# Transposes of half-width column blocks, and their first visit moved ahead of the head sums

## The chip, the cores and the metric

The kernel runs on one core of a Trainium2 chip. The core has a matrix engine (TensorE, in the profile PE, with its weight loads as PEld), three engines for elementwise work (VectorE or DVE, ScalarE or ACT, GpSimd or POOL), a sync engine (SP) that issues DMAs here, and 16 DMA engines. The engines run their own instruction streams in order and wait for each other by semaphores. The metric is the time of one execution on the device in microseconds (us); lower is better. The kernel before takes 361.32 us, the median of three runs (360.48 to 361.93).

## The reference: sliding-window attention with a distance penalty, then a gated feed-forward block

The inputs are q, k and v of 8 batches, 8 heads, 576 tokens and 64 features per head, and three weight matrices. All are float32; the kernel computes in bf16 with float32 accumulation.

```python
scores = scale * np.matmul(q, k.transpose(0, 1, 3, 2))
rel = pos[:, None] - pos[None, :]
bias = slopes[:, None, None] * (-np.abs(rel))[None, :, :]
mask = (rel >= 0) & (rel < 128)
scores = np.where(mask, scores + bias[None], -1e9)
attn = softmax(scores)                      # over the keys
x = matmul(attn, v)                         # to 4608 tokens x 512 features
gelu(x @ w_gate) * (x @ w_val) @ w_out      # 512 -> 1536 -> 512
```

A token sees itself and the 127 tokens before it, so of the 576 x 576 scores only a band is computed.

## The kernel before

**Data and stages.** For each batch the kernel loads q, k and v with tokens on the partitions: `qs` and `ks` hold five blocks of token rows, four of 128 rows and a last one of 64, each 512 wide (8 heads of 64 features). Two buffers of each alternate by batch, `qs[b % 2]`. Scores need the features on the partitions, so TensorE transposes each block by a matmul with the identity: `qT` and `kT` hold, for each of four column groups c (128 columns, two heads), the 576 tokens along the free dimension. From there: score matmuls (`scores`, `scores2`, L209 and L291) into PSUM, exponentials by ACT (L222), multiplication with the precomputed penalty mask by DVE (L225), sums over the keys per head (`sums4`, L430, which reads `T`, a folded copy of the probabilities made by `add`), reciprocals by DVE (L435), and a way of these reciprocals through DRAM to all partitions (`gather` and `spread_dma`, two DMA issues each on ACT's queue, L443 and L449). The values (`values`, L494) are scaled on the way out of PSUM into `xT` (L558).

**The feed-forward part** runs over nine groups g of 512 tokens. For each group and each of twelve column blocks f, `gate_val(g, f)` issues eight matmuls of 512 columns into two PSUM banks (L625); ACT applies the gelu to one (L632) and DVE multiplies it with the other into `hid` (L633). The output matmuls (`out_part`, L662) follow.

**The order.** Everything is issued in the order in which the Python code runs; there is no planner behind it, and each engine keeps that order. The main loop interleaves attention of later batches with the feed-forward part of earlier tokens: in group g the loop over f issues `gate_val(g, f)` and, behind certain f, attention work of batches g + 1 and g + 2; behind the loop stand the steps of `steps(g)`, with the scores of batch g + 2 among the output matmuls. For groups 2 to 5 it goes so: behind f = 3 (4 in group 2) `sums4(g + 1)`, behind f = 5 (6) `gather(g + 1)`, behind f = 6 two transposes of batch g + 2, behind f = 7 (8) `spread_dma(g + 1)`, behind f = 8 the other two transposes, behind f = 9 the loads of q and k of batch g + 3 and of v of batch g + 2, issued by POOL. Batches 2 and 3 are transposed in group 1, behind f = 5, 7 and 11 and twice among the output steps, there directly ahead of score matmuls. Batch 1 has its own code (`transpose`, `transpose_runs`, L154); it transposes 64 columns at a time.

**PSUM banks.** There are eight; `bank()` hands them out in turn. `transposes(b, c)` takes one bank for q and one for k, writes five transposes into each and has the bank copied out by ACT (q) or DVE (k), 576 columns in one copy (L181). TensorE can write a bank again when the copy or the gelu and multiplication that read it are done.

**Forms.** The profile gives each matmul the part of the array that it uses, as rows*columns: 128*128 for the gate and output matmuls, 64*64 for scores and values, 128*32 for the head sums. The transposes of L178 have 128*128 for the blocks of 128 token rows and 64*128 for the last block.

Of the kernel before, what the change touches and what calls it, by code (L numbers as in the profile page):

```python
# [32 lines left out]
def kernel(  # L33
# [10 lines left out]
    nc = tc.nc  # L44
    B, H, S, D = q.shape
# [22 lines left out]
    def bank():  # L68
        return psum.tile([128, 512], FP32, name="ps")
# [11 lines left out]
    ident = consts.tile([128, 128], BF16, name="ident")  # L81
# [20 lines left out]
    def rows(j):  # L102
        return 64 if j == 4 else 128
# [12 lines left out]
    def load_qk(b):  # L116
        load(qs[b % 2], q, b)
        load(ks[b % 2], k, b)

    def load_v(b, js=range(5)):  # L120
        load(vb[b % 2], v, b, js, 64)
# [44 lines left out]
    def transpose(b, what, c, copy):  # L166
        ps = bank().bitcast(BF16)
        for n, lo in ((0, 0), (1, 384)):
            transpose_runs(b, n, what, c, ps[:, lo:576])
        for n, lo in ((0, 0), (1, 384)):  # L170
            untangle(copy, b, n, what, c, c + 1, ps[:, lo:576])

    def transposes(b, c, copies=None):
        for w, (src, dst, copy) in enumerate(zip((qs, ks), (qT, kT), copies or (act, dve))):
            ps = bank().bitcast(BF16)
            for j in range(5):
                n = rows(j)
                nc.tensor.transpose(  # L178
                    out=ps[:, 128 * j:128 * j + n], in_=src[b % 2][0:n, j, 128 * c:128 * c + 128],
                    identity=ident[0:n, 0:n])  # L180
            copy(out=dst[b % 2][:, c, 0:S], in_=ps[:, 0:S])  # L181


# [187 lines left out]
    def add(b, c0, copy=None, what=(0, 1)):  # L371
        hs = slice(2 * c0, 2 * c0 + 4)
        P = Ps[b % 2].rearrange("p h (n y) -> p h n y", y=64)[:, hs]
        to = T.rearrange("p h (n y) -> p h n y", y=64)[:, hs]
        if 0 in what:
            for x in (0, 1):
                half = slice(64 * x, 64 * x + 64)
                nc.vector.tensor_tensor(  # L378
                    out=to[half, :, x:x + 7:2], in0=P[half, :, 0:10:3], in1=P[half, :, 1:11:3],
                    op=ALU.add)  # L380
            nc.vector.tensor_copy(out=to[0:64, :, 8], in_=P[0:64, :, 12])
            nc.vector.tensor_tensor(
                out=to[64:128, :, 8], in0=P[64:128, :, 11], in1=P[64:128, :, 12], op=ALU.add)
        if 1 in what:
            for x in (0, 1):
                half, n = slice(64 * x, 64 * x + 64), 4 - x
                (copy or nc.vector.tensor_copy)(
                    out=to[half, :, x + 1:x + 2 * n:2], in_=P[half, :, 2:3 * n:3])
# [30 lines left out]
    def sums4(b):  # L419
        ps = bank()  # L420
        for s, at in ((0, 0), (1, shape(b, 0)[1])):
            first, w = shape(b, s)
            mms = []
            for h in range(H):
                for x in (0, 1):
                    t = first + w * x
                    g, a = 2 * x + h // 4, 32 * (h % 4)
                    mms.append((g, ones8[:, a:a + 32], T[:, h, t:t + w]))
            for n, (g, lhsT, rhs) in enumerate(in_turn(mms)):
                nc.tensor.matmul(  # L430
                    out=ps[32 * g:32 * g + 32, at:at + w], lhsT=lhsT, rhs=rhs,
                    start=n < 4 and s == 0, stop=True, skip_group_check=True)
        for s, at in ((0, 0), (1, shape(b, 0)[1])):
            first, w = shape(b, s)
            nc.vector.reciprocal(row(b)[:, first:first + w], ps[:, at:at + w])  # L435
# [11 lines left out]
    def spread_dma(b):  # L447
        for i in (0, 1):
            nc.scalar.dma_start(  # L449
                out=recip[b][64 * i:64 * i + 64, :, :],  # L450
                in_=flat[b][i:H:2, :].unsqueeze(0).to_broadcast((64, 4, S)))
# [156 lines left out]
    def gate_val(g, f, lo=0, hi=512, later=None):  # L608
        if g not in hid:
            hid[g] = h_pool.tile([128, NF, 512], BF16, name="hT")  # L610
        t0 = 512 * g % RING
        n = hi - lo

        if n > 256 or lo >= 384:
            pg, pv = bank()[:, 0:n], bank()[:, 0:n]
            order = [(w, ps, c, c == 0) for w, ps in ((wg, pg), (wv, pv)) for c in range(4)]
        else:
            ps = bank()
            pg, pv = ps[:, 0:n], ps[:, n:2 * n]
            order = [(w, ps, c, w is wg and c == 0)  # L620
                     for cs in ((0, 1), (2, 3)) for w, ps in ((wg, pg), (wv, pv)) for c in cs]
        cols = ((0, 256), (256, 512)) if (g, f) in HALVED else ((0, n),)
        for w, ps, c, begins in order:
            for a, e in cols:
                nc.tensor.matmul(  # L625
                    out=ps[:, a:e], lhsT=w[:, c, 128 * f:128 * (f + 1)], rhs=xT[:, c, t0 + lo + a:t0 + lo + e],
                    start=begins and a == 0, stop=(c == 3),
                    skip_group_check=n <= 256 and lo < 384 or len(cols) > 1)

        def act():  # L630
            gl = g_pool.tile([128, 512], BF16, name="gelu")
            nc.scalar.activation(out=gl[:, 0:n], in_=pg, func=AF.Gelu)  # L632
            nc.vector.tensor_tensor(out=hid[g][:, f, lo:hi], in0=pv, in1=gl[:, 0:n],  # L633
                                    op=ALU.mult)

        if later is None:
            act()
        else:
            later.append(act)
# [77 lines left out]
    for h in (0, 2, 4, 6):  # L717
        for w, src in ((0, q), (1, k)):
            (nc.scalar if w and h == 0 else nc.sync).dma_start(  # L719
                out=raw[w][h // 4].rearrange("p (h x) -> p h x", h=4)[:, h % 4:h % 4 + 2, :],  # L720
                in_=src[0][h:h + 2, 0:384, :].rearrange("h (p r) d -> p h (r d)", r=3))
# [42 lines left out]
    def masks_of_last_blocks(lo, hi):  # L764
        nc.vector.tensor_copy(out=emask[:, lo:hi, 192:384], in_=emask[:, lo:hi, 0:192])
        nc.vector.tensor_copy(out=emask[:, lo:hi, 384:512], in_=emask[:, lo:hi, 0:128])
        for x, at in ((0, 128), (1, 0)):
            half = slice(64 * x, 64 * x + 64)
            nc.vector.tensor_copy(out=emask[half, lo:hi, 512:576], in_=emask[half, lo:hi, at:at + 64])
# [67 lines left out]
    for do in inverse_a:  # L837
        do[1]()
    dve(out=pairs1.rearrange("p x (h d) -> p h x d", d=64),
        in_=vb[1].rearrange("p j x -> p (j x)")[:, 0:1536].rearrange(  # L840
            "p (h x d) -> p h x d", h=H, x=3))
# [46 lines left out]
    for n in range(4):  # L888
        nc.gpsimd.dma_start(
            out=wo[:, 3 * n:3 * n + 3, :],  # L890
            in_=moe_w_out[384 * n:384 * n + 384, :].rearrange("(c p) f -> p c f", p=128))
# [32 lines left out]
    for g in range(NG):  # L924
        for f in range(9 if g == 0 else 0, NF):
            gate_val(g, f)
            if g == 1 and f in (5, 7):
                transposes(2, f - 5)
                transposes(2, f - 4)
            if g == 1 and f == 11:  # L930
                transposes(3, 0)
                transposes(3, 1)
                nc.gpsimd.tensor_copy(out=mark, in_=hid[g][0:1, f, 0:2])
                load_qk(4)
                load_v(3)
            if 2 <= g < B - 2 and f in (6, 8):
                transposes(g + 2, f - 6)
                transposes(g + 2, f - 5)
            if g == 2 and f == 2:
                add(3, 2, act, (1,))  # L940
            if g == 0 and f == 10:
                masks_of_last_blocks(0, 8)
            if g == 0 and f == 9:
                for c in range(4):
                    for w in (0, 1):
                        transpose(1, w, c, (act, dve)[w])
            if 2 <= g < B - 1:
                if f == (4 if g == 2 else 3):
                    sums4(g + 1)
                if f == (6 if g == 2 else 5):  # L950
                    gather(g + 1)
                if f == (8 if g == 2 else 7):
                    spread_dma(g + 1)
                if f == 9 and g + 2 < B:

                    nc.gpsimd.tensor_copy(out=mark, in_=hid[g][0:1, f, 0:2])  # L956
                    if g + 3 < B:
                        load_qk(g + 3)
                    load_v(g + 2)
        if g == 0:  # L960
            nc.gpsimd.memset(Ps[0][:, :, 0:64], 0.0)
        for item in steps(g):
            if isinstance(item, int):
                out_part(g, item)
            else:
                RUN[item[0]](*item[1:])
        store()
        if g == 0:
            load_qk(3)
            load_v(2)  # L970
# [30 lines left out]
```

## Time and profile before

| | before |
|---|---|
| median of three runs | 361.32 us |
| lowest and highest | 360.48 and 361.93 us |
| the profiled execution | 361.49 us |
| its span, first to last instruction | 359.7 us |
| TensorE busy | 349.9 us, 97% |
| DVE, ACT, POOL busy | 57%, 51%, 29% |
| granted TensorE clock | 1.0 in the whole span |
| instructions of L178 (matmuls) | 240 |

The profile is one execution. Its page gives each engine's busy time and the chain of work that ended last, followed back from the end. A matmul's duration in the profile holds its way through the array, and matmuls overlap, so the pace of TensorE is read from the starts of instructions that follow each other and not from durations. The timeline lists instructions in order of time, with those of the same line and operation drawn together: start, length, engine, line, operation, tiles, form, shape, number. A few matmul records are missing from the trace.

### The profile page before, as it was taken

What the parts mean: (1) busy time and instruction counts of PE and PEld (TensorE: products, weight loads), DVE (VectorE), ACT (ScalarE), POOL (GpSimd) and SP (SyncE); (2) the same over time, 40 slices, a digit from 0 to 9 for tenths busy, and PEclk for the clock granted to TensorE, in tenths of its full rate; (3) what the DMA queues carried; (4) which work ended last, traced back from release to release, by engine and by line L of the source; (5) the groups of instructions that cost most, each with busy time, mean ns of one, the idle gap of its engine ahead of it and who ended that gap; (6) DMA issues with size and microseconds to landing.
All of it is one profiled execution on the core that took longest, in us unless ns stands there. A gap on an engine that the chain in (4) does not pass through costs nothing.

```text
span 359.7 us, 8537 instructions
## 1 busy us (share of the span) xinstructions
PE 349.9 (97%) x3508; PEld 184.7 (51%) x3556; DVE 203.4 (57%) x382; ACT 184.4 (51%) x340; POOL 105.6 (29%) x139
## 2 busy tenths in 40 slices
PE   8999999999999999999999999999999999999996
PEld 6667556555654555454545554455544544444444
DVE  7887865445789546944596458844694413302420
ACT  7964786447696437544473439253753123313322
POOL 6965689406700086004900192004000000000000
PEclk9999999999999999999999999999999999999999
DMA  8999999908950099219990599049203320011002
GB/s 210 171 197 191 200 187 187 124 2 52 162 107 2 5 194 189 64 23 135 170 122 5 131 138 181 3 104 105 81 31 69 95 89 2 0 58 60 0 28 90
DMA packets 118043, 35.65 MB, mean 99 GB/s; under 512 B 101716, under 2 KB 110964, under 8 KB 118004
## 3 DMA queue, kind: packets, MB, share of 16 engines
q0 software_dynamic: 107456, 18.10, 65.2%
q1 hardware_dynamic: 7232, 10.75, 8.5%
q10 hardware_dynamic: 3316, 6.25, 7.9%
q8 instruction: 28, 0.46, 0.5%
q14 instruction: 11, 0.09, 0.1%
HBM read 43.65 MB, written 9.53 MB: 148 GB/s over the span
## 4 chain that ended last, share of the span: by engine, by line
PE 94%; DMA 1%; issue 1%; DVE 1%; ACT 1%; SPq 0%; DVEq 0%
PE ps L625 52%; PE ps L662 24%; PE ps L178 6%; PE ps L494 5%; PE ps L291 2%; PE ps L682 2%; PE ps L209 1%; DMA qs<-in_q_dram 1%; PE ps L430 1%; PE ps L698 1%; PE ps L154 1%; ACT P L222 0%; SPq L719 0%; DVE xT L530 0%; DVE qT L162 0%
## 5 line engine op out<-in xcount | busy, mean ns | idle before, releaser
L633 DVE TENSOR_TENSOR hT<-ps,gelu 128x512 bf16<-128x512 f32 (+3 forms) x117 | 73.8, 646 | 97.6 <-PE ps L625 91.3
L632 ACT ACTIVATE gelu<-ps 128x512 bf16<-128x512 f32 (+3 forms) x117 | 65.1, 564 | 98.5 <-PE ps L625 96.2
L625 PE MATMUL ps<-xT,wg 128*128 128x512 bf16 (+4 forms) x460 | 112.1, 361 | 0.8
L625 PE MATMUL ps<-xT,wv 128*128 128x512 bf16 (+4 forms) x460 | 111.2, 361 | 0.4
L662 PE MATMUL ps<-wo,hT 128*128 128x512 bf16 x374 | 87.6, 380 | 2.1 <-issue 1.4
L625 PEld LDWEIGHTS <-wv 128*128 128x128 bf16 x472 | 45.0, 98 | 48.7
L625 PEld LDWEIGHTS <-wg 128*128 128x128 bf16 x472 | 43.5, 98 | 45.8
L662 PEld LDWEIGHTS <-hT 128*128 128x128 bf16 x396 | 37.0, 98 | 43.3
L222 ACT ACTIVATE P<-ps 128x512 bf16<-128x512 f32 (+1 forms) x108 | 51.3, 583 | 3.9 <-PE ps L209 3.6
L225 DVE TENSOR_TENSOR P<-P,emask 128x768 bf16<-128x768 bf16 x60 | 31.2, 556 | 19.5 <-ACT P L222 17.7
L667 ACT COPY osb<-ps 128x512 f32<-128x512 f32 x27 | 15.9, 588 | 51.3 <-PE ps L662 51.3
L112 POOL DMA_DIRECT2D vb<-in_v_dram x40 | 34.0, 902 | 2.9 <-DMA wo<-in_moe_w_out_dram 1.0
L956 POOL COPY mark<-hT 1x2 bf16<-1x2 bf16 x4 | 0.7, 174 | 108.4 <-DVE hT L633 108.4
L112 POOL DMA_DIRECT2D qs<-in_q_dram x30 | 25.5, 870 | 4.9 <-DMA wo<-in_moe_w_out_dram 2.7
L112 POOL DMA_DIRECT2D ks<-in_k_dram x30 | 25.4, 893 | 0.3 <-PE ps L625 0.3
L181 ACT COPY qT<-ps 128x576 bf16<-128x576 bf16 x22 | 14.0, 638 | 9.8 <-PE ps L178 9.8
L494 PE MATMUL ps<-P,vb 64*64 64x192 bf16 (+2 forms) x752 | 17.7, 221 | 0.6 <-issue 0.4
L558 DVE TENSOR_TENSOR xT<-ps,rb 128x512 bf16<-128x512 f32 (+3 forms) x34 | 14.7, 502 | 4.6 <-PE ps L494 4.6
L494 PEld LDWEIGHTS <-vb 64*64 64x64 bf16 x752 | 14.7, 107 | 4.0 <-issue 3.0
L181 DVE COPY kT<-ps 128x576 bf16<-128x576 bf16 x24 | 11.0, 457 | 5.7 <-PE ps L178 5.1
L378 DVE TENSOR_TENSOR T<-P 64x1024 bf16<-64x1024 bf16 x20 | 13.7, 686 | 0.6
L178 PE MATMUL ps<-ident,ks 128*128 128x128 bf16 (+1 forms) x120 | 12.7, 218 | 0.0
(95 smaller groups left out, 238.0 us busy)
## 6 DMA issues: line engine op xcount, KB each, us to landing
out_dram<-osb SPq DMA_DIRECT2D x35, 256.0 KB, 3.1
rb<-rd ACTq DMA_DIRECT2D x10, 576.0 KB, 6.4
vb<-in_v_dram POOLq DMA_DIRECT2D x32, 128.0 KB, 6.3
qs<-in_q_dram POOLq DMA_DIRECT2D x24, 128.0 KB, 4.5
ks<-in_k_dram POOLq DMA_DIRECT2D x24, 128.0 KB, 6.1
wo<-in_moe_w_out_dram POOLq DMA_DIRECT2D x4, 384.0 KB, 12.3
wg<-in_moe_w_gate_dram POOLq DMA_DIRECT2D x5, 256.0 KB, 8.4
wv<-in_moe_w_val_dram POOLq DMA_DIRECT2D x5, 256.0 KB, 8.9
```

The source lines that it names most:

```text
L112: nc.gpsimd.dma_start(out=t[at:at + n, j, :].rearrange("p (h d) -> p h d", h=H), in_=src[b][:, 128 * j:128 * j + n, :].rearrange("h p d -> ...
L178: nc.tensor.transpose(out=ps[:, 128 * j:128 * j + n], in_=src[b % 2][0:n, j, 128 * c:128 * c + 128], identity=ident[0:n, 0:n])
L181: copy(out=dst[b % 2][:, c, 0:S], in_=ps[:, 0:S])
L222: nc.scalar.activation(out=dst, in_=src, func=AF.Exp, scale=0.125)
L225: nc.vector.tensor_tensor(out=dst, in0=dst, in1=m, op=ALU.mult)
L494: mm = nc.tensor.matmul(out=out, lhsT=lhsT, rhs=prob(b)[half, c, i, col:col + q1 - q0], start=all(t[2] != u for t in todo[:n]), stop=True, ...
L558: nc.vector.tensor_tensor(out=xT[:, c, at:at + e - a], in0=src, in1=recip[b][:, c, a:e], op=ALU.mult)
L625: nc.tensor.matmul(out=ps[:, a:e], lhsT=w[:, c, 128 * f:128 * (f + 1)], rhs=xT[:, c, t0 + lo + a:t0 + lo + e], start=begins and a == 0, st ...
L632: nc.scalar.activation(out=gl[:, 0:n], in_=pg, func=AF.Gelu)
L633: nc.vector.tensor_tensor(out=hid[g][:, f, lo:hi], in0=pv, in1=gl[:, 0:n], op=ALU.mult)
L662: nc.tensor.matmul(out=acc[g], lhsT=hid[g][:, f, 128 * t:128 * (t + 1)], rhs=wo[:, f, :], start=(f == 0), stop=(f == NF - 1))
L667: (nc.vector.tensor_copy if g < B - 2 and t in by_dve.get(g, (0,)) else nc.scalar.copy)(out=osb, in_=acc[g])
```

## The change

The transposes of batches 2 to 7 take 64 columns each instead of 128: two instructions per block of token rows, whose outputs go to the partitions 0 to 63 and 64 to 127 of the same bank. Their forms are 128*64 for the blocks of 128 rows and 64*64 for the last one. A call of `transposes` issues 20 of them instead of 10; banks and copies stay.

In groups 2 to 5 the first of the two visits, column groups 0 and 1 of batch g + 2, is issued behind f = 4 in group 2 and behind f = 3 in groups 3 to 5, where it was f = 6. In the order of the code that is directly ahead of `sums4(g + 1)`. The second visit stays behind f = 8.

```diff
             for j in range(5):
                 n = rows(j)
-                nc.tensor.transpose(
-                    out=ps[:, 128 * j:128 * j + n], in_=src[b % 2][0:n, j, 128 * c:128 * c + 128],
-                    identity=ident[0:n, 0:n])
+                for i in (0, 1):
+                    at = 128 * c + 64 * i
+                    nc.tensor.transpose(
+                        out=ps[64 * i:64 * i + 64, 128 * j:128 * j + n],
+                        in_=src[b % 2][0:n, j, at:at + 64], identity=ident[0:n, 0:n])
             copy(out=dst[b % 2][:, c, 0:S], in_=ps[:, 0:S])
...
-            if 2 <= g < B - 2 and f in (6, 8):
-                transposes(g + 2, f - 6)
-                transposes(g + 2, f - 5)
+            first = 4 if g == 2 else 3
+            if 2 <= g < B - 2 and f in (first, 8):
+                for c in ((0, 1) if f == first else (2, 3)):
+                    transposes(g + 2, c)
```

## The prediction

> **What bounds the kernel now.** I read the page first, then the chain in order of time, then the timeline of TensorE (PE) around each kind of transpose. The page says that TensorE is the bound, and that the changed line holds a visible share of the chain:
>
> ```profile
> PE 349.9 (97%) x3508; PEld 184.7 (51%) x3556; DVE 203.4 (57%) x382; ACT 184.4 (51%) x340; POOL 105.6 (29%) x139
> ...
> PE ps L625 52%; PE ps L662 24%; PE ps L178 6%; PE ps L494 5%; PE ps L291 2%; PE ps L682 2%; PE ps L209 1%; DMA qs<-in_q_dram 1%; PE ps L430 1%; PE ps L698 1%; PE ps L154 1%; ACT P L222 0%; SPq L719 0%; DVE xT L530 0%; DVE qT L162 0%
> ```
>
> L178 is the changed transpose: 6%, or some 22 us. A TensorE that never waits can be shortened only by giving it less to do, or the same work at a closer pace. Two stretches of its timeline show that pace. First, one visit of the old transposes (20 instructions, four sets of five) between gate matmuls; each line is one set, its first number its start:
>
> ```profile
> 68.12 0.59 PE L625 MATMUL ps<-xT,wv 128*128 128x512 bf16 x2
> 68.55 0.52 PE L178 MATMUL ps<-ident,qs 128*128 128x128 bf16 x5
> 69.00 0.53 PE L178 MATMUL ps<-ident,ks 128*128 128x128 bf16 x5
> 69.46 0.53 PE L178 MATMUL ps<-ident,qs 128*128 128x128 bf16 x5
> 69.92 0.53 PE L178 MATMUL ps<-ident,ks 128*128 128x128 bf16 x5
> 70.39 0.39 PE L625 MATMUL ps<-xT,wg 128*128 128x512 bf16 x1
> ```
>
> The same line, narrower: the fifth instruction of a set works on 64 rows (form 64*128) and stands alone between full ones (128*128):
>
> ```profile
> 68.72 0.35 PE L178 MATMUL ps<-ident,qs 128*128 128x128 bf16 x2
> ...
> 68.87 0.20 PE L178 MATMUL ps<-ident,qs 64*128 64x64 bf16 x1
> 69.00 0.29 PE L178 MATMUL ps<-ident,ks 128*128 128x128 bf16 x2
> ```
>
> Second, batch 1, which already transposes 64 columns at a time (L154, form 128*64, pairs side by side in the array):
>
> ```profile
> 36.28 0.38 PE L625 MATMUL ps<-xT,wv 128*128 128x512 bf16 x1
> 36.59 0.45 PE L154 MATMUL ps<-ident,qs 128*64 128x128 bf16 x10
> 36.87 0.42 PE L154 MATMUL ps<-ident,ks 128*64 128x128 bf16 x10
> ...
> 37.12 0.42 PE L154 MATMUL ps<-ident,qs 128*64 128x128 bf16 x10
> 37.38 0.42 PE L154 MATMUL ps<-ident,ks 128*64 128x128 bf16 x10
> ```
>
> Ten L154 instructions take 0.255 us, five L178 ones 0.462 us. It is tempting to read a saving of 0.2 us a set from that. The narrow lines say otherwise. Full transposes start 56 ns apart, but the 64-row one starts 151 ns after its neighbour (68.72 to 68.87), and the next full one 132 ns after it (its own 64 columns stream in 27 ns). So a set is 0.224 us of streaming and some 0.2 us of two changes of form. L154 looks fast because all ten instructions keep one form (its short rows are 96, and count as 128). In the changed code the fifth block still has 64 rows, so the changes stay.
>
> **The price of a change of form.** Reading starts in the trace to the nanosecond, every change costs the same. From the last 512-column matmul into 128*64 (L154), 64*64 (L291) or 128*32 (L430) it is 309 ns against the usual 216: 93. From 128*128 into 64*128 it is 151 less 56: 95. Out of 64*64 it is 122 less 27: 95; out of 64*128 into 64*64, 121 less 27: 94. Besides, the first instructions in a new form last longer, and what follows comes later by as much: 243 against 219 ns in 128*64 (+24), 214 against 190 in 64*64 (+23), 200 against 191 in 64*128 (+9), 231 against 220 in 128*128 (+11).
>
> **Part one: 64 columns each.** 48 sets (six batches, four column groups, q and k) become ten instructions each: 240 more matmuls and as many weight loads. In L154 the second of a pair starts 3 to 5 ns after the first and pairs stand 56 ns apart, so four pairs stream in the same 0.224 us as four full transposes; its weight loads (106 to 113 ns against 91 to 100) overlap. Nothing is won or lost in streaming.
> A set today: 67 + 56 + 56 + 151 + 132 = 462 ns. A set after: 79 + 56 + 56 (starts of the pairs, the first late by its 24) + 152 (into 64*64) + 4 (second of the small pair) + 27 + 23 + 95 (that pair streams late, then the change back) = 492 ns. That is +30 ns, times 48: +1.44 us. No row shows 64*64 straight after 128*64; the rows for rows alone (95), for columns alone (93 to 94) and for both (93) are equal, so I take 95. Its bounds: +7 ns a set if the late start of the small pair does not lengthen the change back (+0.3 us), +48 ns if each change costs 9 more for the longer loads (+2.3 us); below nothing is the rival further down.
> A visit today begins with full transposes after full gate matmuls, without a change (68.33 to 68.55); after, it begins with one. There are 13 visits (8 of batches 4 to 7, 3 of 20 in the gate loop of group 1, 2 of 10 among its output steps): 13 x 93 = +1.21 us, and 13 x 11 = +0.14 because their first set is spared the slow restart today.
> Three visits of group 1 end in score matmuls in 64*64 (L209 at 84.44, 87.76, 90.43). The new small pair is already in that form, so a change and a slow start fall away: 3 x 0.118 = -0.35 us.
> The copies out of the bank (L181, 576 columns) are the same; ACT and DVE have as much to do as before.
>
> Here a rule of the Trainium skill speaks against the edit. TensorEngine Tiling (Array Packing), section Performance Considerations, puts a cost of about 60 cycles on each matmul and advises against splitting what is small already. At the 2.4 GHz that TensorE: Matmul & The Clock Gate gives, I estimate 25 ns for each of 240 more, and by it the sum below would be 6 us higher, near 369 us. The row differs: with two halves side by side the second one costs 4 ns.
>
> **Part two: the first visit of batches 4 to 7 moves.** In group g it went behind gate step 6; now it goes behind step 4 (g = 2) or 3, directly ahead of the head sums (L430, form 128*32) of the next batch. Its 40 matmuls, 40 loads, 2 ACT and 2 DVE copies keep their number; no DMA issue of POOL or SP moves. On TensorE the visit's last change and the sums' first become one: the 93 into the sums and the 10 of slow gate restart go, 4 x 0.103 = -0.41 us.
> What could wait: (a) Loads. In group 4 the moved visit starts near 189.4, in groups 2, 3, 5 near 113.3, 150.5, 228.6; the DMA engines have gone quiet before each (last two numbers of a row: packet time as a share of the 16 engines' time, and GB/s):
>
> ```profile
> 104.00:113.00 9.00, 8.95 (x81) 4.32 (x71) 8.50 (x18) 8.35 (x15) 0.00 (x0) 1.00 0.08 29
> ...
> 147.00:150.50 3.50, 3.50 (x17) 1.42 (x16) 3.40 (x8) 1.20 (x2) 0.00 (x0) 1.00 0.00 1
> ...
> 185.00:189.40 4.40, 4.40 (x21) 1.84 (x19) 4.25 (x9) 2.13 (x4) 0.00 (x0) 1.00 0.03 7
> ...
> 224.00:228.60 4.60, 4.60 (x22) 1.94 (x20) 4.45 (x10) 2.28 (x5) 0.00 (x0) 1.00 0.01 2
> ```
>
> (b) Banks and DVE. Group 2 is the tight one, as DVE comes out of a backlog there:
>
> ```profile
> 112.03 3.08 DVE L633 TENSOR_TENSOR hT<-ps,gelu 128x512 bf16<-128x512 f32 x5
> ...
> 115.03 1.96 DVE L435 RECIPROCAL r<-ps 128x128 f32<-128x128 f32 x2
> ...
> 118.86 1.65 ACTq L443 DMA_DIRECT2D rd<-r  x2
> ```
>
> The visit's fourth bank is freed by the third of these five (about 113.9), and its set starts near 114.8: 0.9 us of slack. The two kT copies (0.46 each) now stand ahead of the reciprocals; DVE is free for them at 115.1 and done at 116.0, when the sums, 2 us later than today, end too. The reciprocals end near 118.0 instead of 117.0, and the gather (L443), which ACT issues behind the gelu of step 6, went at 118.86 anyway. In group 3 the gather is due behind a gelu that moves with the visit from 153.9 to 155.9, and the reciprocals end near 155.3; it landed 1 us after its issue, and the spread that needs it goes near 159.3, behind step 7, as before. All covered: 0, with bounds from nothing to the rival's price.
>
> **Sum.** 1.44 + 1.21 + 0.14 - 0.35 - 0.41 = +2.0 us on the profiled execution of 361.49 us (span 359.7 and 1.8 around it): 363.5. The median of the runs is 0.17 lower; on it, 363.3.
>
> **Rivals.**
> *Cheap changes of rows* (the other side: faster). If going from 128*64 to 64*64, both split by columns, needed no change of form, a set would be 0.224 + 0.031 = 0.255 us, 0.207 less than today: -9.9, and with the entries about -9 us: 352.4. For it: no row shows this pair of forms. Against it: rows alone cost 95 between full-width forms. The whole change breaks even where each of the 96 changes costs 21 ns less than 95, and is faster by over 0.5% where it costs under about 55. The Trainium skill's Tiling page (Key Properties) lets every change of mode drain the array and names no exception; no run here shows this pair.
> *No late small pair*: the changes cost 95, the first-of-form delay does not add up: 0.3 instead of 1.44, so +0.9 us: 362.2, no measurable change.
> *The moved visit makes a wait*: recips late, gather late, ACT held, gelu late, TensorE out of banks. It decides where the gather slips by more than the 2 us or so between its landing and the spread; 1 to 2 us in each of four groups: 367 to 371. For it: DVE's backlog at 112; against it: the slacks above.
> *Loads unhidden after a change*: one 107 ns load more at each of 96 changes, 373. Against it: both first pairs (L154, L291) start 2 to 4 ns apart.
>
> **Chances.** Forecast 0.62, no late pair 0.13, cheap rows 0.13, moved wait 0.07, unhidden loads 0.05. Measurement tells about 0.5% (1.8 us) from nothing; the forecast's own range, +0.9 to +3.0, has some six tenths above that. Slower: 0.38 + 0.12 = 0.50; same: 0.24 + 0.13 = 0.37; faster 0.13. The range goes from "no late pair" less the 0.84 us by which the lowest run lies under the median, to the upper price of a set (+2.9) with the same on top: 361.4 to 365.0; it leaves out cheap rows and most of the two slow ones.
>
> **What would show it.** L178 sets at a period of 0.49 us with the small pair some 150 ns behind its neighbour and the next set 145 ns behind that; 0.31 us into a visit; sums starting about 0.15 us behind the moved visit; no TensorE idle at L430 or the gate after it. A set at 0.26 us means cheap rows and a time near 352; L443 or L449 holding ACT back means the moved wait. I am wrong above all if the one pair of forms that this trace lacks costs something else than 95 ns.

## The result and the profile after

The changed kernel takes 363.29 us (median of six runs, 362.69 to 364.01), the kernel before beside it 361.0 us (six runs, 360.34 to 361.93). The ratio is 1.0065 with a 95% interval of 1.0045 to 1.0086: slower by 2.3 us, between 1.6 and 3.1. The profiled execution took 363.08 us, with a span of 361.3.

The page after: TensorE's busy time and the chain, with the changed transposes now under L180 (the edit moves later lines by two or three).

```profile
PE 355.3 (98%) x3796; PEld 186.2 (52%) x3796; DVE 204.0 (56%) x382; ACT 184.2 (51%) x340; POOL 106.2 (29%) x139
...
PE ps L627 52%; PE ps L664 24%; PE ps L180 7%; PE ps L496 5%; PE ps L293 2%; PE ps L684 2%; PE ps L211 1%; DMA qs<-in_q_dram 1%; PE ps L432 1%; PE ps L700 1%; PE ps L154 1%; ACT P L224 0%; SPq L721 0%; DVE qT L162 0%; ACT rb L578 0%
```

The transposes hold 7% of the chain instead of 6%; nothing else has taken more. (The matmul counts of two traces do not compare: records are missing from the one before.) The same visit as before, in the timeline of TensorE; a line is a set, now of ten instructions:

```profile
67.68 0.59 PE L627 MATMUL ps<-xT,wv 128*128 128x512 bf16 x2
68.20 0.56 PE L180 MATMUL ps<-ident,qs 128*64 128x128 bf16 x10
68.69 0.56 PE L180 MATMUL ps<-ident,ks 128*64 128x128 bf16 x10
69.18 0.56 PE L180 MATMUL ps<-ident,qs 128*64 128x128 bf16 x10
69.67 0.56 PE L180 MATMUL ps<-ident,ks 128*64 128x128 bf16 x10
70.17 0.39 PE L627 MATMUL ps<-xT,wg 128*128 128x512 bf16 x1
```

A set takes 0.49 us where it took 0.46. The last gate matmul starts at 67.89 (67.68 and 0.215), so 0.31 us pass before the first transpose; before it was 0.22. Narrower, at the end of the first set:

```profile
68.55 0.22 PE L180 MATMUL ps<-ident,qs 64*64 64x64 bf16 x2
68.69 0.25 PE L180 MATMUL ps<-ident,ks 128*64 128x128 bf16 x2
```

A block now takes two instructions, one per 64-column half; the small pair is the two halves of the 64-row block. To the nanosecond, the small pair starts 149 ns after the second half of its neighbour, in all 48 sets (149 to 150), and where a set follows, it starts 143 to 145 ns after the small pair's second half. These are the two changes of form. The moved visit, in group 2, with the head sums (L432) behind it:

```profile
112.96 0.59 PE L627 MATMUL ps<-xT,wv 128*128 128x512 bf16 x2
113.49 0.56 PE L180 MATMUL ps<-ident,qs 128*64 128x128 bf16 x10
...
114.96 0.56 PE L180 MATMUL ps<-ident,ks 128*64 128x128 bf16 x10
115.45 0.68 PE L432 MATMUL ps<-T,ones 128*32 128x128 bf16 x32
116.07 0.39 PE L627 MATMUL ps<-xT,wg 128*128 128x512 bf16 x1
```

The sums begin 143 ns behind the visit's last instruction, and no waiting stands between them. The whole list of what TensorE's matmuls waited for (time, number, longest) has no transpose, no sum and no gate matmul in it:

```profile
PE ps L74 <- DVE zeros L710: 1.0, 1, 1.0
PE ps L779 <- DVE qs L761: 0.4, 1, 0.4
PE ps L211 <- DVE kT L162: 0.2, 1, 0.2
PE ps L496 <- issue: 0.2, 1, 0.2
PE ps L496 <- ACT P L224: 0.2, 1, 0.2
```

Adding up the trace: a visit between gate matmuls goes from 2.053 us (last gate matmul's start to the next one's) to 2.275, +0.222, six times. The four moved visits with their sums take 2.889 us, measured the same way. Apart they took 2.051 and 0.925; as one such interval is now a plain 0.216 between two gate matmuls, and one slow gate restart of 0.010 falls away, this is +0.119 each. The three visits of group 1 that end in scores take 0.04 to 0.10 us more, up to the first matmul behind the scores (for one of them a record missing in the trace before is allowed for). Together this is some +2.0 us, inside the measured interval.

### The profile page after: what moved, and what is told of

It reads as the page before. It is cut to its first block, busy times and chain, and to the rows that moved or that the text cites. A ratio compares the mean times of both kernels' runs of the same rounds, so it can differ in the third digit from the quotient of the medians.

```text
span 361.3 us, 9064 instructions
## 1 busy us (share of the span) xinstructions
PE 355.3 (98%) x3796; PEld 186.2 (52%) x3796; DVE 204.0 (56%) x382; ACT 184.2 (51%) x340; POOL 106.2 (29%) x139
## 4 chain that ended last, share of the span: by engine, by line
PE 96%; DMA 1%; DVE 1%; ACT 1%; SPq 0%; issue 0%; DVEq 0%
PE ps L627 52%; PE ps L664 24%; PE ps L180 7%; PE ps L496 5%; PE ps L293 2%; PE ps L684 2%; PE ps L211 1%; DMA qs<-in_q_dram 1%; PE ps L432 1%; PE ps L700 1%; PE ps L154 1%; ACT P L224 0%; SPq L721 0%; DVE qT L162 0%; ACT rb L578 0%
## 5 line engine op out<-in xcount | busy, mean ns | idle before, releaser
L627 PE MATMUL ps<-xT,wv 128*128 128x512 bf16 (+4 forms) x472 | 112.8, 361 | 0.0
L664 PE MATMUL ps<-wo,hT 128*128 128x512 bf16 x396 | 90.3, 380 | 0.0
L180 PE MATMUL ps<-ident,qs 128*64 128x128 bf16 (+1 forms) x240 | 13.5, 223 | 0.0
```

Of the source, the lines that this page charges most:

```text
L180: nc.tensor.transpose(out=ps[64 * i:64 * i + 64, 128 * j:128 * j + n], in_=src[b % 2][0:n, j, at:at + 64], identity=ident[0:n, 0:n])
L627: nc.tensor.matmul(out=ps[:, a:e], lhsT=w[:, c, 128 * f:128 * (f + 1)], rhs=xT[:, c, t0 + lo + a:t0 + lo + e], start=begins and a == 0, st ...
L664: nc.tensor.matmul(out=acc[g], lhsT=hid[g][:, f, 128 * t:128 * (t + 1)], rhs=wo[:, f, :], start=(f == 0), stop=(f == NF - 1))
```

## The experiments

The theory: TensorE pays about 95 ns for each change of form, and some 10 to 24 ns for the first instructions of the new one; neither the number of transposes nor the place of the visit costs anything. The rivals: 240 more matmuls cost time each; the 64-row transposes are slow by themselves; the moved visit makes a wait.

### The two parts apart

The 64-column transposes alone, visits behind f = 6 and 8:

```diff
-                nc.tensor.transpose(
-                    out=ps[:, 128 * j:128 * j + n], in_=src[b % 2][0:n, j, 128 * c:128 * c + 128],
-                    identity=ident[0:n, 0:n])
+                for i in (0, 1):
+                    at = 128 * c + 64 * i
+                    nc.tensor.transpose(
+                        out=ps[64 * i:64 * i + 64, 128 * j:128 * j + n],
+                        in_=src[b % 2][0:n, j, at:at + 64], identity=ident[0:n, 0:n])
```

> The 64-column transposes alone, with the visits where they were before. Theory (changes of form): sets at a period of 0.49 us, 0.31 us into each of the 13 visits, and the head sums pay their own 0.31 us again, so +2.7 us on the kernel before, 0.4 us more than both parts together. Rival (the moved visit makes a wait that is part of the +2.3 us): less than +2.3 us here. Rival (each of 240 more matmuls costs some 10 ns): +2.4 us as well, but then the pairs in a set stand further apart than 56 ns.

Measured: 364.02 us against 361.42, ratio 1.0064 (1.0047 to 1.0081), +2.3 us with an interval that holds the expected 2.7 (1.7 to 2.9). The head sums stand alone again, between gate matmuls:

```profile
113.18 1.03 PE L627 MATMUL ps<-xT,wv 128*128 128x512 bf16 x4
114.14 0.68 PE L432 MATMUL ps<-T,ones 128*32 128x128 bf16 x32
114.75 0.39 PE L627 MATMUL ps<-xT,wg 128*128 128x512 bf16 x1
```

The last of the four gate matmuls starts at 113.83, the sums 0.31 us later: the change that the moved visit saves. All of the loss is in this part; that it is 0.4 us more than the loss of both parts together cannot be told from these times, whose intervals are 1.2 and 1.5 us wide, only from the trace. In its trace pairs still start 56 ns apart (80 for the first two behind a change), so the added matmuls lengthen the stream of a set by nothing but the 3 to 4 ns between the last two halves.

The move alone, with 128 columns:

```diff
-            if 2 <= g < B - 2 and f in (6, 8):
-                transposes(g + 2, f - 6)
-                transposes(g + 2, f - 5)
+            first = 4 if g == 2 else 3
+            if 2 <= g < B - 2 and f in (first, 8):
+                for c in ((0, 1) if f == first else (2, 3)):
+                    transposes(g + 2, c)
```

> The moved first visit alone, with transposes of 128 columns. Theory: the change out of the visit and the change into the sums become one, 4 x 0.1 = 0.4 us less than before, no TensorE wait at the sums, the gather or the gate step behind. Rival (the moved visit makes a wait): +1 us or more, with ACT or TensorE idle near the sums of groups 2 to 5.

Measured: 361.0 us against 361.42, ratio 0.9984 (0.9972 to 0.9995): faster by 0.2 to 1.0 us, with the expected 0.4 inside. In its timeline the sums follow the last set directly, 130 ns behind the 64-row transpose, in all four groups:

```profile
114.82 0.53 PE L178 MATMUL ps<-ident,ks 128*128 128x128 bf16 x5
115.28 0.68 PE L430 MATMUL ps<-T,ones 128*32 128x128 bf16 x32
115.90 0.39 PE L625 MATMUL ps<-xT,wg 128*128 128x512 bf16 x1
```

No wait of TensorE appears near them. The rival of a wait falls: the move by itself is a small gain.

### No change of form inside a visit

The last block is transposed with 96 rows in place of 64. The profile counts 96 rows with the 128-row form, as the transposes of batch 1 show. The rows 64 to 95 hold old data of batch 1 or zeros, and their 32 output columns are never copied out. Once on the changed kernel (64 columns), once on the kernel before (128 columns):

```diff
             for j in range(5):
-                n = rows(j)
+                n = 96 if j == 4 else 128
...
+    for t in (qs[0], ks[0]):
+        nc.gpsimd.memset(t[64:96, 4, :], 0.0)
     nc.gpsimd.memset(T[64:128, :, 0:64], 0.0)
```

> The changed kernel, but the last block of token rows is transposed with 96 rows (64 and 32 that nobody reads), which are counted as the 128-row form; two small memsets on POOL give those rows a value. No change of form is left inside a visit. Theory: a set is four pairs at 56 ns and one at 42 ns, 0.27 us instead of 0.49; a visit of 20 pairs keeps one change in and one out; 8.9 us less than the changed kernel, about 354.4 us. Rival (the 240 added matmuls cost the time): the sets stay near 0.45 us or above and the time near 363.

> The kernel before with 96 rows in the last block, 128 columns. No change of form inside a visit, and none into it or out of it beside gate matmuls. Theory: sets at 0.27 us against 0.462, about 9 us less than before, 352 us, and 2 to 3 us less than the 64-column kernel with 96 rows, from the changes into and out of its visits alone; the sets of both have the same period. Rival (added matmuls cost some 10 ns each): the same distance between the two, but with longer sets in the 64-column one. Rival (the 64-row transpose is slow by itself, not the change): the sets get shorter by a few ns only.

Measured: 64 columns with 96 rows 355.45 us against 361.42, ratio 0.9829 (0.9810 to 0.9848); 128 columns with 96 rows 352.66 us, ratio 0.9751 (0.9731 to 0.9770). The first is 8.5 us under the changed kernel by the two ratios (7.8 between the medians), where 8.9 was expected; the second 8.3 to 9.7 us under the one before. Their visits, first 64 columns, then 128:

```profile
68.85 0.81 PE L627 MATMUL ps<-xT,wv 128*128 128x512 bf16 x3
69.59 0.46 PE L180 MATMUL ps<-ident,qs 128*64 128x128 bf16 x10
69.89 0.43 PE L180 MATMUL ps<-ident,ks 128*64 128x128 bf16 x10
70.16 0.43 PE L180 MATMUL ps<-ident,qs 128*64 128x128 bf16 x10
70.43 0.43 PE L180 MATMUL ps<-ident,ks 128*64 128x128 bf16 x10
70.80 0.39 PE L627 MATMUL ps<-xT,wg 128*128 128x512 bf16 x1
```

```profile
68.07 1.03 PE L625 MATMUL ps<-xT,wv 128*128 128x512 bf16 x4
68.93 0.43 PE L178 MATMUL ps<-ident,qs 128*128 128x128 bf16 x5
69.20 0.43 PE L178 MATMUL ps<-ident,ks 128*128 128x128 bf16 x5
69.47 0.43 PE L178 MATMUL ps<-ident,qs 128*128 128x128 bf16 x5
69.74 0.43 PE L178 MATMUL ps<-ident,ks 128*128 128x128 bf16 x5
70.01 0.38 PE L625 MATMUL ps<-xT,wg 128*128 128x512 bf16 x1
```

Ten half-width instructions and five full-width ones take the same 0.27 us a set. What sets the two visits apart is the edge: the half-width one pays 0.31 us to enter (last gate matmul at 69.28), 23 ns for its slow first set and 0.14 us to leave, the full-width one enters at the usual 0.22. Over 13 visits that is 13 x 0.116 to enter and 6 x 0.104 to leave to gate matmuls, 2.1 us; measured are 2.8 us between the medians, and the two intervals (each 1.4 us wide) leave 2.1 open. So the added matmuls are free. These two runs change the rows together with the form; whether a 64-row transpose is slow by itself is decided by the next two, which keep every shape.

### Fewer changes and more changes, the same instructions

If the change of form is what costs, its number must set the time with every shape left as it is. Fewer: the kernel before, with the full blocks of a visit first and its last blocks together behind them. A call now takes all column groups of its visit.

```diff
-    def transposes(b, c, copies=None):
-        for w, (src, dst, copy) in enumerate(zip((qs, ks), (qT, kT), copies or (act, dve))):
-            ps = bank().bitcast(BF16)
-            for j in range(5):
-                n = rows(j)
-                nc.tensor.transpose(...)
-            copy(out=dst[b % 2][:, c, 0:S], in_=ps[:, 0:S])
+    def transposes(b, cs, copies=None):
+        work = [(c, src, dst, copy, bank().bitcast(BF16)) for c in cs
+                for src, dst, copy in zip((qs, ks), (qT, kT), copies or (act, dve))]
+        for js in (range(4), (4,)):
+            for c, src, dst, copy, ps in work:
+                for j in js:
+                    n = rows(j)
+                    nc.tensor.transpose(...)
+        for c, src, dst, copy, ps in work:
+            copy(out=dst[b % 2][:, c, 0:S], in_=ps[:, 0:S])
```

> The kernel before, transposes of 128 columns and 64-row last blocks as they were, but each visit issues the full blocks of all its banks first and its last blocks after them: two changes of form in a visit instead of eight, the same 240 matmuls with the same shapes; the copies come at the end of the visit. Theory (each change costs some 0.1 us): a visit of 20 takes 16 x 56 + 95 + 4 x 28 + 105 = 1.21 us instead of 1.84, 11 of them, and two of ten save 0.2 each: -7.3 us, 354 us. Rival (a 64-row transpose is slow by itself, or the short set at the end of a bank waits for its copy): within 2 us of before.

Measured: 354.52 us against 360.89, ratio 0.9813 (0.9791 to 0.9836), 5.9 to 7.5 us less. The visit, with the four 64-row transposes now side by side:

```profile
68.84 0.39 PE L180 MATMUL ps<-ident,qs 128*128 128x128 bf16 x4
...
69.51 0.39 PE L180 MATMUL ps<-ident,ks 128*128 128x128 bf16 x4
69.83 0.20 PE L180 MATMUL ps<-ident,qs 64*128 64x64 bf16 x1
69.87 0.19 PE L180 MATMUL ps<-ident,ks 64*128 64x64 bf16 x1
69.89 0.19 PE L180 MATMUL ps<-ident,qs 64*128 64x64 bf16 x1
69.92 0.19 PE L180 MATMUL ps<-ident,ks 64*128 64x64 bf16 x1
70.05 0.61 PE L628 MATMUL ps<-xT,wg 128*128 128x512 bf16 x2
```

1.21 us, as worked out. The last blocks start 29 to 40 ns apart: the 64-row transpose is short where its form does not change, and it was slow only because its form stood alone. One score matmul of group 1 now starts some 0.3 us late (the one before it at 86.28, it at 86.66), behind an exponential of ACT (L225) that ends at 86.61; the rest of the small gap to the expected 7.3 us lies inside the interval.

More: the changed kernel, with a full-height pair between the two halves of the last block, so that a set changes form four times.

```diff
-            for j in range(5):
+            for j, halves in ((0, (0, 1)), (1, (0, 1)), (2, (0, 1)), (4, (0,)), (3, (0, 1)), (4, (1,))):
                 n = rows(j)
-                for i in (0, 1):
+                for i in halves:
```

> The changed kernel with the two halves of the last block parted by a pair of full-height halves, so that each set changes form four times instead of twice; matmuls, shapes, copies and places as in the changed kernel. Theory: one more excursion a set costs 149 + 27 + 23 + 95 + 24 less the 56 of streaming that was there anyway, 0.26 us, times 48: +12.6 us on the changed kernel, 376 us. Rival (the time comes from the number of matmuls): no difference from the changed kernel.

Measured: 375.54 us, ratio 1.0404 (1.0386 to 1.0423) to the kernel before, 12.2 us over the changed kernel. The same 480 matmuls take 0.75 us a set:

```profile
68.62 0.82 PE L180 MATMUL ps<-ident,qs 128*64 128x128 bf16 x10
69.37 0.82 PE L180 MATMUL ps<-ident,ks 128*64 128x128 bf16 x10
70.12 0.82 PE L180 MATMUL ps<-ident,qs 128*64 128x128 bf16 x10
```

That is 0.26 us more than in the changed kernel, times 48: 12.5 us. With four changes a set instead of two, and in the kernel before with two a visit instead of eight, the order of the instructions alone moves the time by what the changes cost.

## Why the prediction was right

*The price of a change of form*: right. The one pair of forms that the trace before lacked, 128*64 to 64*64, costs what the others cost: 149 ns from the neighbour's second half less 53 to 56 of streaming, 93 to 96, and 143 less 27 and the small pair's late 23, 93, on the way back. The rival of cheap changes of rows is gone.

What fills the 95 ns stays open. The weight loads tell a part of it. Before, the first load of a visit starts 0.21 us ahead of its matmul (68.55); after, it starts with it (68.20), behind the gap, and the loading path stood idle for 0.42 us:

```profile
68.34 0.62 PEld L178 LDWEIGHTS <-qs 128*128 128x128 bf16 x5
...
68.20 0.45 PEld L180 LDWEIGHTS <-qs 128*64 128x64 bf16 x10 [0.42 <-issue]
```

So in these records no weights are loaded ahead across a change: the small pair's loads start 1 to 2 ns ahead of their matmuls in all 48 sets, those inside a form 53 to 55 ns. The length of the load is not the price, for loads into 64*128 take 91 to 93 ns and into 64*64 102 to 103, and the two changes cost the same.

*A set at 492 ns*: 491 in the trace. The step that carried the risk, that the late start of the small pair lengthens the change back, held; its rival of 362.2 us falls. So does the one of one more unhidden weight load at each change, since halves start 3 to 4 ns apart behind every change.

*Entries* (into a visit, from the last matmul before it): 13 of 13 at 309 to 310 ns, as priced. *Scores*: in the three visits of group 1 the L211 matmuls follow the small pair without a change, 0.01 us behind it. *Sums*: four of five follow a visit directly, at 143 to 144 ns; the move alone brought its small gain.

*The moved visit hides its waits*: right, and close where it was called tight. In group 2, timeline of DVE and ACT after:

```profile
112.38 3.08 DVE L635 TENSOR_TENSOR hT<-ps,gelu 128x512 bf16<-128x512 f32 x5
...
115.38 0.81 DVE L183 COPY kT<-ps 128x576 bf16<-128x576 bf16 x2
...
116.19 1.97 DVE L437 RECIPROCAL r<-ps 128x128 f32<-128x128 f32 x2
...
118.87 1.66 ACTq L445 DMA_DIRECT2D rd<-r  x2
```

The reciprocals end at 118.16 (118.0 foretold) and the gather goes at 118.87, behind its gelu, as before; 0.7 us were left.

*The sum*: +2.0 us foretold, +2.0 by the trace, +2.3 (1.6 to 3.1) by the runs. That the median of 363.29 meets the 363.3 foretold to a hundredth is luck: beside it the kernel before took 361.0 and not 361.32, and the rise was 2.3 and not 2.0. *The Trainium skill's rule on splitting* (TensorEngine Tiling (Array Packing), Performance Considerations): read as a cost that each matmul adds, its 60 cycles would have made 6 us by my estimate, and the runs show no such cost. With both halves in flight the second starts 3 to 4 ns after the first, and the sets with 96 rows take 0.27 us at either width. The section's own example, that one column takes as long as 60, speaks of the shortest matmuls; those here stream 64 columns or more. The same page's statement that a change of mode drains the engine (Key Properties) fits the runs; they give the price, and do not show the drain itself.

## What to carry to other kernels

Where TensorE hardly ever waits, as here, count the changes of form and not only the instructions: each one cost about as much as two full transposes (95 ns and a slow start against 56 ns each). A ragged last block that falls into another form was cheaper with padding rows that keep the form (full width and 96 rows took 352.66 us, 2.5% less than before), or collected with its like (354.52 us, 1.9% less). Before copying a faster-looking variant from elsewhere in a kernel, look at why it is fast: batch 1's half-width transposes were quick because their short blocks had 96 rows, not because of the 64 columns.

## What I had not expected of the hardware

That splitting the width costs nothing in streaming was foretold; that it comes out so exactly was not: a set takes 0.27 us with five full-width transposes and with ten half-width ones, although a half-width weight load lasts longer in the profile (102 to 110 ns against 91 to 100). And that 32 rows which nobody reads make a transpose cheaper: of a set of the kernel before, 0.462 less 4 x 0.056 = 0.238 us went to its one 64-row transpose and the changes around it; with 96 rows it is 0.27 less 0.224, some 0.05.
